# MLP matmul steps cut into 32-row pieces beside single score tiles, with other margins in the order and another head

## The chip, the cores and the metric

One core of one Trainium2 chip. The time is microseconds (us) of device time of one execution. The kernel before has a median of 706.06 us (704.78 to 706.14, three runs). In each set of runs below the kernel before was run beside the others on the same chip; its medians there were 705.9 to 706.1 us. The mean clock granted to TensorE differs a little from run to run, and the time with it: of eleven runs of the kernel before, the one at clock 1.000 took 704.58 us and the three at 0.990 took 707.2 to 707.5 us. So I compare medians first, and runs of equal clock where that matters.

## The reference

```python
def reference(A_x, A_wqkv, A_wo, B_x, B_w1, B_b1, B_w2, B_b2):   # [cut]
    xn = layernorm(A_x)                      # 1 x 2048 x 512, bf16
    # A: softmax attention of layernorm'd rows, 32 heads of width 16
    q, k, v = split(xn @ wqkv)
    a = softmax(q @ k.T / 4) @ v             # per head, 2048 x 2048 scores
    A = merge_heads(a) @ wo
    # B: an MLP over the token axis, 2048 -> 1376 -> 2048
    h = layernorm(xn)
    u = gelu(einsum("bsd,sf->bdf", h, w1) + b1)
    B = transpose(einsum("bdf,fs->bds", u, w2) + b2)
    return A_x + A + B
```

The scores are the bulk of it: 32 x 2048 x 2048 exponentials.

## The kernel before

The kernel writes its own static instruction order. A list scheduler with modelled durations picks, again and again, the operation that can start first, and appends it to the order of its engine. At run time every engine works through its order in sequence and waits for semaphores. So a wrong model does no harm to correctness; it puts a waiting operation in front of a ready one.

A *score tile* is 128 keys x 1024 (two heads x 512 queries): two matmuls on two row groups of 32 rows each, into two banks of PSUM, the memory that TensorE writes its results to. There are three such PSUM slots. The tile is exponentiated either by ScalarE or by VectorE, the latter with an integer trick of four terms. A *PV group* (exponentials times the values V) is four matmuls on the four column groups of 32 columns. An *MLP step* has the same form. Row-tiled scores and column-tiled PV and MLP work therefore alternate in phases.

```python
def score_specs(n):                      # [cut] two row groups, S phase
    r = 2 * (n % 2) + i                  # rows 0,1 or 2,3
    matmul(bank(2 * s_ + i), lhsT=KT[32*r:32*r+32, T, ...], rhs=QT[32*r:32*r+32, b % 4, :],
           tile_position=(32 * r, 0))
def pv_specs(item, first, last):         # [cut] four column groups, C phase; 1 (ScalarE) or 4 (VectorE) of them per tile
    matmul(bank(PV_BANK)[32*c:32*c+32, ...], lhsT=vt[:, off:off+32], rhs=buf(p, ...), tile_position=(0, 32 * c))
def ext_mm(dst_rows, lhs_of, rhs, reads, start, stop, name):   # [cut] one MLP or projection step, C phase
    for c in range(4):
        matmul(bank(EX_BANK)[32*c:32*c+w, :], lhsT=lhs_of(32*c, 32*c+w), rhs=rhs, tile_position=(0, 32 * c))

# [cut] a score on VectorE: one tensor_scalar from PSUM, then three shifted copies (1 on VectorE, 2 on GpSimd)
# [cut] the head
warm_up(N_WARM, 5)
pool.memset(v17_main[:, :, 16:17], 1.0)          # the 2.3 us GpSimd memset
ln_stats(0); ...; ln_rstd(1, 2); ln_stats(3)     # ln_rstd runs on GpSimd
for t in range(NPRE): ln_norm(t)                 # bf16 tensor_scalar on VectorE
late_memsets()                                   # four small GpSimd memsets
for t in range(NPRE): transpose_pe(t, TB[t])
```

The softmax here doesn't subtract the row's maximum and nothing guards it: scores larger than these inputs give would overflow.

## Time and profile before

I cut the span at two marks: the start of the first exponential of a score tile, and the start of the last PV matmul.

| stretch | us |
|---|---|
| head: to the first exponential | 12.95 |
| main: first exponential to last PV matmul | 680.07 |
| tail: last PV matmul to the end of the span | 11.26 |
| span of the profiled run | 704.3 |

First, the page of the kernel before: busy time of each engine (PE is TensorE, PEld its weight loads, DVE VectorE, ACT ScalarE, POOL GpSimd), then the costliest groups (line, engine, operation, operands, count, then busy us and mean ns of one, then the engine's idle time just before and what ended it).

```profile
PE 688.5 (98%) x12808; PEld 325.6 (46%) x12808; DVE 607.0 (86%) x879; ACT 680.4 (97%) x744; POOL 391.3 (56%) x666
...
L737 ACT ACTIVATE pT<-ps 128x1024 bf16<-128x1024 f32 x522 | 515.4, 1151 | 3.8 <-PE ps L713 3.2
L713 PE MATMUL ps<-QT,KT 32*128 32x512 bf16 x2048 | 291.0, 384 | 5.0 <-ACT pT L737 3.0
L748 DVE TENSOR_SCALAR pT<-ps 128x1024 int16<-128x1024 f32 x207 | 252.9, 1222 | 32.7 <-PE ps L713 23.6
...
L748 DVE TENSOR_SCALAR x_sb<-ps 128x1024 int16<-128x1024 f32 x92 | 112.4, 1222 | 15.3 <-PE ps L713 10.8
```

207 + 92 = 299 of the 1024 score tiles go to VectorE. VectorE waits 23.6 + 10.8 = 34.4 us for them.

The table by stage of the kernel before (stretch, length, then busy us and instructions of PE, PEld, DVE, ACT, POOL, then the clock, the DMA share and GB/s):

```profile
100.00:600.00 500.00, 496.57 (x9574) 234.38 (x9570) 441.45 (x591) 498.99 (x544) 289.75 (x482) 1.00 0.18 40
600.00:690.00 90.00, 89.31 (x1636) 40.57 (x1628) 78.95 (x106) 89.21 (x99) 52.35 (x89) 1.00 0.21 51
```

ScalarE is full: 498.99 of 500 us. VectorE is at 441.45 / 500 = 88.3%.

The timeline of the kernel before (start, length, engine, line, operation; in brackets how long the engine stood idle before it and what released it), at the head, in two score phases near 303 us, and at the tail:

```profile
2.72 2.29 POOL L626 MEMSET V<- 128x512 bf16 x1
...
6.55 2.28 DVE L522 TENSOR_SCALAR hx<-x_sb,mv 128x512 bf16<-128x512 bf16 x4
...
10.14 1.48 PE L601 MATMUL ps<-xnT,wq_sb 128*128 128x128 bf16 x12
...
12.95 3.77 ACT L737 ACTIVATE pT<-ps 128x1024 bf16<-128x1024 f32 x4 [0.81 <-PE ps L713]
...
302.99 0.48 PE L713 MATMUL ps<-QT,KT 32*128 32x512 bf16 x4
303.40 0.40 PE L780 MATMUL ps<-pT,V 128*32 128x256 bf16 x8
...
304.06 0.39 PE L713 MATMUL ps<-QT,KT 32*128 32x512 bf16 x2
304.38 0.29 PE L780 MATMUL ps<-pT,V 128*32 128x256 bf16 x4
...
693.12 2.55 PE L810 MATMUL ps<-gT_sb,wblk 128*32 128x512 bf16 x44
...
695.67 0.42 DVE L1043 TENSOR_TENSOR oT<-ps,oC 128x256 bf16<-128x256 f32 x1
...
698.41 1.03 PE L1059 MATMUL ps<-wo_t,oT 128*128 128x512 bf16 x4
```

Three things are to be seen. A phase of one score tile (x2 matmuls) takes 304.38 - 304.06 = 0.32 us until the next column-tiled work, and one of two tiles (x4) takes 0.41 us here. At the tail, TensorE works off eleven MLP steps (x44) after the last PV matmul. And the head ends at 12.95 us.

### The profile page before, as it was taken

The page shows a single profiled execution, that of the slowest core. Times are in us where ns is not written, and L with a number is a line of the kernel's source. Part 1 is how long each engine was busy: PE and PEld are TensorE (multiplying, and loading weights), DVE is VectorE, ACT ScalarE, POOL GpSimd, SP SyncE. Part 2 cuts the span into 40 slices and gives each one's busy share as a digit, 9 for nine tenths or more (in the row PEclk, how much of TensorE's full clock was granted, in tenths as well). Part 3 has the DMA queues.
Part 4 walks back from the last instruction along what each step waited for, and adds up shares of the span by engine and source line. Part 5 has one row for each costly group of instructions (what it writes and reads, how often), then busy time and mean ns, then how long its engine had stood idle before and what let it go on. Part 6 is the DMA issues. An engine that isn't in the chain of part 4 may idle for free.

```text
span 704.3 us, 29187 instructions
## 1 busy us (share of the span) xinstructions
PE 688.5 (98%) x12808; PEld 325.6 (46%) x12808; DVE 607.0 (86%) x879; ACT 680.4 (97%) x744; POOL 391.3 (56%) x666
## 2 busy tenths in 40 slices
PE   7999999999999999999999999999999999999998
PEld 4533544444444454444444454444544444445444
DVE  6968889888897889989889998979899888988886
ACT  5999999999999999999999999999999999999993
POOL 5535446565564636556565674546556564665551
PEclk9999999999999999999999999999999999999999
DMA  7103200221002200211221023112221121222211
GB/s 210 32 19 69 51 23 14 52 49 27 15 14 53 48 23 18 43 36 36 49 42 44 19 47 72 48 39 53 54 55 35 43 66 41 53 55 54 48 43 47
DMA packets 85727, 32.31 MB, mean 46 GB/s; under 512 B 67424, under 2 KB 85600, under 8 KB 85600
## 3 DMA queue, kind: packets, MB, share of 16 engines
q1 hardware_dynamic: 85168, 30.05, 18.4%
q8 instruction: 100, 1.64, 1.0%
q10 hardware_dynamic: 432, 0.39, 0.2%
q14 instruction: 27, 0.22, 0.1%
HBM read 21.76 MB, written 2.35 MB: 34 GB/s over the span
## 4 chain that ended last, share of the span: by engine, by line
PE 73%; ACT 19%; DVE 3%; issue 2%; SPq 2%; POOL 1%; DVEq 0%; DMA 0%; POOLq 0%
PE ps L780 27%; PE ps L713 27%; PE ps L810 15%; ACT pT L737 13%; ACT x_sb L737 4%; SPq L404 2%; PE ps L859 1%; DVE pT L748 1%; ACT gT_sb L914 1%; PE ps L619 0%; DVE oT L1006 0%; PE ps L563 0%; PE ps L550 0%; DVE x_sb L748 0%; POOL V L626 0%
## 5 line engine op out<-in xcount | busy, mean ns | idle before, releaser
L737 ACT ACTIVATE pT<-ps 128x1024 bf16<-128x1024 f32 x522 | 515.4, 1151 | 3.8 <-PE ps L713 3.2
L713 PE MATMUL ps<-QT,KT 32*128 32x512 bf16 x2048 | 291.0, 384 | 5.0 <-ACT pT L737 3.0
L748 DVE TENSOR_SCALAR pT<-ps 128x1024 int16<-128x1024 f32 x207 | 252.9, 1222 | 32.7 <-PE ps L713 23.6
L754 POOL INT64_ADD pT<-pT x307 | 185.6, 613 | 147.1 <-DVE pT L757 80.9
L780 PE MATMUL ps<-pT,V 128*32 128x256 bf16 x4632 | 237.9, 275 | 0.9 <-ACT pT L737 0.6
L737 ACT ACTIVATE x_sb<-ps 128x1024 bf16<-128x1024 f32 x203 | 221.8, 1159 | 1.1 <-PE ps L713 0.9
L713 PEld LDWEIGHTS ps<-QT,KT 32*128 32x128 bf16 x2048 | 86.5, 91 | 179.2 <-ACT pT L737 80.6
L780 PEld LDWEIGHTS ps<-pT,V 128*32 128x32 bf16 x4632 | 109.9, 96 | 68.0 <-issue 52.1
L748 DVE TENSOR_SCALAR x_sb<-ps 128x1024 int16<-128x1024 f32 x92 | 112.4, 1222 | 15.3 <-PE ps L713 10.8
L780 PE MATMUL ps<-x_sb,V 128*32 128x256 bf16 x1856 | 115.1, 275 | 0.3 <-ACT x_sb L737 0.3
L754 POOL INT64_ADD pT<-x_sb x128 | 77.4, 613 | 56.8 <-DVE pT L757 32.6
L754 POOL INT64_ADD x_sb<-pT x114 | 69.4, 613 | 44.8 <-DVE pT L757 31.0
L757 DVE TENSOR_SCALAR pT<-pT 128x1024 int16<-128x1024 int16 x149 | 63.4, 428 | 4.5
L780 PE MATMUL ps<-pT,VM 128*32 128x256 bf16 x884 | 61.2, 274 | 0.0
L810 PE MATMUL ps<-hx,wblk 128*32 128x512 bf16 x688 | 60.5, 384 | 0.0
L810 PE MATMUL ps<-gT_sb,wblk 128*32 128x512 bf16 (+1 forms) x704 | 58.4, 383 | 0.7 <-DVE hx L948 0.7
L780 PEld LDWEIGHTS ps<-x_sb,V 128*32 128x32 bf16 x1856 | 47.3, 96 | 24.2 <-issue 18.1
L754 POOL INT64_ADD x_sb<-x_sb x58 | 35.3, 613 | 28.4 <-DVE pT L757 8.1
L757 DVE TENSOR_SCALAR pT<-x_sb 128x1024 int16<-128x1024 int16 x66 | 27.9, 424 | 2.1
L810 PEld LDWEIGHTS ps<-hx,wblk 128*32 128x32 bf16 x688 | 16.2, 94 | 24.1 <-issue 21.1
L780 PEld LDWEIGHTS ps<-pT,VM 128*32 128x32 bf16 x884 | 23.6, 97 | 6.6 <-issue 6.1
L810 PEld LDWEIGHTS ps<-gT_sb,wblk 128*32 128x32 bf16 (+1 forms) x704 | 16.3, 95 | 20.8 <-issue 16.1
(105 smaller groups left out, 397.4 us busy)
## 6 DMA issues: line engine op xcount, KB each, us to landing
wblk<-in_B_w_dram SPq DMA_DIRECT2D x10, 512.0 KB, 4.6
wblk<-in_B_w_dram SPq DMA_DIRECT2D x16, 320.0 KB, 3.6
oC<-OT SPq DMA_DIRECT2D x248, 16.0 KB, 1.8
denb<-rden_scratch SPq DMA_DIRECT2D x124, 32.0 KB, 2.0
xr<-in_A_x_dram SPq DMA_DIRECT2D x16, 128.0 KB, 2.3
dcomp<-OT SPq DMA_DIRECT2D x124, 2.0 KB, 1.8
QT<-Qall SPq DMA_DIRECT2D x120, 16.0 KB, 1.8
out_dram<-osb SPq DMA_DIRECT2D x14, 128.0 KB, 1.9
```

Source lines behind the costliest of these rows:

```text
L404: return eng.dma_start(dst, src)
L713: specs.append(dict(eng="pe", fn=lambda e, r=r, bk=bk: e.matmul(bank(bk), lhsT=KT[32 * r:32 * r + 32, T, 128 * kt:128 * (kt + 1)], rhs=QT[ ...
L737: return [dict(eng="act", fn=lambda e: e.activation(buf(pbuf[n]), ps[:, s_ * 1024:(s_ + 1) * 1024], ACTF.Exp, scale=LN2_128), reads=[("ban ...
L748: return dict(eng="dve", fn=lambda e: e.tensor_scalar(buf_i(w), ps[:, s_ * 1024:(s_ + 1) * 1024], IBIAS, 0.0, ALU.add, ALU.max), reads=[(" ...
L754: return dict(eng=eng, fn=lambda e: e.int64_add(buf_i(o).bitcast(I64), buf_i(w).bitcast(I64), SHIFTS[k] * 0x0001000100010001), reads=[("pT ...
L757: return dict(eng=eng, fn=lambda e: e.tensor_scalar(buf_i(o), buf_i(w), float(SHIFTS[k]), 1.0, ALU.add, ALU.mult), reads=[("pT", w)], writ ...
L780: specs.append(dict(eng="pe", fn=lambda e, c=c, h=h, i=i, off=off: e.matmul(bank(PV_BANK)[32 * c:32 * c + 32, 256 * par:256 * par + 256], ...
L810: specs.append(dict(eng="pe", fn=lambda e, c=c, w=w: e.matmul(bank(EX_BANK)[32 * c:32 * c + w, :], lhsT=lhs_of(32 * c, 32 * c + w), rhs=rh ...
L859: specs.append(dict(eng="pe", fn=lambda e, ct=ct, c=c, i=i, t=t: e.matmul(bank(EX_BANK)[32 * c:32 * c + 32, 128 * i:128 * (i + 1)], lhsT=x ...
L914: yield "act", [dict(eng="act", fn=lambda e, ap=ap: e.activation(ap, ap, ACTF.Gelu_apprx_tanh), reads=[("gT", f) for f in fts], writes=[(" ...
```

## The change

Intent: in a phase with a single score tile two of the four row groups idle. A 32-row piece of an MLP step, a quarter of it, can run there. Four pieces replace one column-tiled step. Around it the order gets other margins, another head, and earlier due times for the output tasks.

```diff
-N_WARM = 11
+N_WARM = 13
+N_MID = (1, 1, 1, 2)              # warm-up matmuls between the transposes
-PE_SWITCH = 0.11
+PE_SWITCH = 0.10
-DMA_I = 0.6
-DMA_L = 3.5
+DMA_I = 0.65
+DMA_L = 3.0
+DMA_SLACK = 0.8                   # with EXT_SLACK = 0.2, PV_SLACK = 0.1: the "margins"
-D_LATE = 1.0
+D_LATE = 0.5                      # when a score tile is wanted for VectorE: the "lateness setting"
 [cut]
+            def piece(r, begin, end=False):
+                rs = slice(32 * r, 32 * r + 32)
+                return [dict(eng="pe", fn=lambda e: e.matmul(
+                    bank(EX_BANK)[0:dst_rows, :], lhsT=lhs_of(0, dst_rows)[rs], rhs=rhs[rs],
+                    start=begin, stop=end, tile_position=(32 * r, 0)), ... name="pc", cost=("S", (r,), 0.214))]
 [cut] pieces(): at the end of a row-tiled phase, one row group of the task's last step goes in if it
       ends with the scores; pieces of different row groups are ordered by TensorE's own semaphore;
       a step is opened for pieces only while its task has at least PIECE_MIN = 6 steps left
-        sc.add("pool", lambda e: e.memset(v17_main[:, :, 16:17], 1.0), ...)      # was before ln_stats(0)
         ln_stats(3)
+        sc.add("pool", lambda e: e.memset(v17_main[:, :, 16:17], 1.0), ...)      # now before the ln_norm loop
         for t in range(NPRE):
             ln_norm(t)
 [cut]
+        for i, z in enumerate(ext_tasks):                                        # the "due times"
+            if z[2] == "fin":
+                due = min(z[1], FIN_END - (NT - 1 - z[4][1]) * FIN_STEP)
+                ext_tasks[i] = (min(z[0], due - 30),) + (due,) + z[2:]
 [cut]
+                    if nm in ("ut", "fin") and any(z[2] == "qt" and z[0] < next_n + Q_GUARD for z in ext_tasks):
+                        continue                                                 # the "query guard"
```

With the query guard goes a rule that the DMAs of query rows are issued before others. A few more small edits are cut.

More of the change, by code (lines that the diff above doesn't have):

```diff
@@ L48 @@
 NPRE = 4
-N_WARM = 11
+N_WARM = 13
+N_MID = (1, 1, 1, 2)
 SEM = 0.05
-PE_SWITCH = 0.11
+PE_SWITCH = 0.10
+PIECE_MIN = 6
+PIECE_OPEN = 1
+HOLD_MAX = 2.0
 PE_LAT = 0.40
@@ L59 @@
 EV_I, EV_L = 0.61, 0.69
-DMA_I = 0.6
-DMA_L = 3.5
+DMA_I = 0.65
+DMA_L = 3.0
+DMA_SLACK = 0.8
+EXT_SLACK = 0.2
+PV_SLACK = 0.1
+GEN_SLACK = 0.0
 SH_I, SH_L = 0.62, 0.70
@@ L68 @@
 D_STEAL = 0.3
-D_LATE = 1.0
+D_LATE = 0.5
 P_KEEP = 4
 DEAD_SLACK = 0.1
+PAIR_WAIT = 0.0
 PORT_SLACK = 0.5
@@ L76 @@
 Q_LEAD = 52
+Q_GUARD = 8
 KV_LEAD = 16
@@ L82 @@
 EX_EARLY = 10
+FIN_END = 985
+FIN_STEP = 18
 GELU_GAP = 16
@@ L124, in __init__ @@
         self.pe_tiles = {}
+        self.phase = 0
+        self.pieces = {}
         self.pe_log = []
@@ L147, in _deps, with ready, piece_ready @@
         return deps
-    def ready(self, eng, reads, writes, dma=False):
+    def ready(self, eng, reads, writes, dma=False, slack=0.0, dma_slack=0.0):
         t = 0.0
         for d in self._deps(eng, reads, writes, dma):
-            t = max(t, d.t1 + (SEM if d.eng != eng or d.is_dma else 0.03))
+            t = max(t, d.t1 + (SEM + (dma_slack if d.is_dma else slack) if d.eng != eng or d.is_dma else 0.03))
         return t
+    def piece_ready(self, r):
+        return max([p.t1 + SEM for q, p in self.pieces.items() if q != r] + [0.0])
     def port_time(self, eng, t):
@@ L174, in _time @@
                 self.pe_tiles = {}
+                self.phase += 1
             for x in tiles:
@@ L208, in add @@
         deps.discard(op)
+        if name == "pc":
+            for r, p in self.pieces.items():
+                if r != cost[1][0]:
+                    deps.add(p)
         if port is None:
             port = eng == "pool" and not dma
-        self._time(op, cost, self.ready(eng, reads, writes, dma), port)
+        rdy = self.ready(eng, reads, writes, dma)
+        if name == "pc":
+            rdy = max(rdy, self.piece_ready(cost[1][0]))
+            self.pieces[cost[1][0]] = op
+        self._time(op, cost, rdy, port)
         if port and eng == "pool" and self.port_op is not None:
@@ L625, in bass_parallel_sum__softmax_full_mha__mixer_token_mlp__prompt_kernel @@
         warm_up(N_WARM, 5)
-        sc.add("pool", lambda e: e.memset(v17_main[:, :, 16:17], 1.0), writes=[("Vone",)], cost=(0.5, 0.6))
         ln_stats(0)
@@ L632, in bass_parallel_sum__softmax_full_mha__mixer_token_mlp__prompt_kernel @@
         ln_stats(3)
+        sc.add("pool", lambda e: e.memset(v17_main[:, :, 16:17], 1.0), writes=[("Vone",)], cost=(2.28, 2.33))
         for t in range(NPRE):
@@ L639, in bass_parallel_sum__softmax_full_mha__mixer_token_mlp__prompt_kernel @@
             transpose_pe(t, TB[t])
+            warm_up(N_MID[t], 5)
         for t in range(NPRE):
@@ L802, in bass_parallel_sum__softmax_full_mha__mixer_token_mlp__prompt_kernel, with ext_mm, step @@
         w_hold = {}
-        def ext_mm(dst_rows, lhs_of, rhs, reads, start, stop, name):
-            specs = []
-            for c in range((dst_rows + 31) // 32):
-                w = min(32, dst_rows - 32 * c)
-                specs.append(dict(eng="pe", fn=lambda e, c=c, w=w: e.matmul(
-                    bank(EX_BANK)[32 * c:32 * c + w, :], lhsT=lhs_of(32 * c, 32 * c + w), rhs=rhs,
-                    start=start, stop=stop, tile_position=(0, 32 * c)),
-                    reads=reads, writes=[("bank", EX_BANK)], name=name, cost=("C", (c,), 0.214)))
-            return specs
+        def ext_mm(dst_rows, lhs_of, rhs, reads, stop, name):
+            def step(begin, end=False):
+                specs = []
+                for c in range((dst_rows + 31) // 32):
+                    w = min(32, dst_rows - 32 * c)
+                    specs.append(dict(eng="pe", fn=lambda e, c=c, w=w: e.matmul(
+                        bank(EX_BANK)[32 * c:32 * c + w, :], lhsT=lhs_of(32 * c, 32 * c + w), rhs=rhs,
+                        start=begin, stop=end, tile_position=(0, 32 * c)),
+                        reads=reads, writes=[("bank", EX_BANK)], name=name, cost=("C", (c,), 0.214)))
+                return specs
+            def piece(r, begin, end=False):
+                rs = slice(32 * r, 32 * r + 32)
+                return [dict(eng="pe", fn=lambda e: e.matmul(
+                    bank(EX_BANK)[0:dst_rows, :], lhsT=lhs_of(0, dst_rows)[rs], rhs=rhs[rs],
+                    start=begin, stop=end, tile_position=(32 * r, 0)),
+                    reads=reads, writes=[("bank", EX_BANK)], name="pc", cost=("S", (r,), 0.214))]
+            return step, piece, stop
         have = {("q", 0), ("q", 1)} | {("k", 0, c) for c in range(4)} | {("v", 0, c) for c in range(4)}
@@ L826, in task_qt @@
         def task_qt(qb, T):
-            for ct in range(NCT):
-                yield "pe", ext_mm(128, lambda a, z, ct=ct: wq_sb[:, ct, 128 * T + a:128 * T + z],
+            yield "steps", [ext_mm(128, lambda a, z, ct=ct: wq_sb[:, ct, 128 * T + a:128 * T + z],
                                    xnT[:, ct, 512 * qb:512 * (qb + 1)],
                                    [("wq", T)] + [("xnT", t) for t in range(4 * qb, 4 * qb + 4)],
-                                   ct == 0, ct == NCT - 1, "qt")
+                                   ct == NCT - 1, "qt") for ct in range(NCT)]
             yield "ev", [dict(eng="dve", fn=lambda e: e.tensor_scalar(Qall[:], bank(EX_BANK), QSCALE, None, ALU.mult),
@@ L843, in task_kt @@
         def task_kt(T, c):
-            for ct in range(NCT):
-                yield "pe", ext_mm(128, lambda a, z, ct=ct: wkv_sb[:, ct, 128 * T + a:128 * T + z],
+            yield "steps", [ext_mm(128, lambda a, z, ct=ct: wkv_sb[:, ct, 128 * T + a:128 * T + z],
                                    xnT[:, ct, 512 * c:512 * (c + 1)],
                                    [("wkv", 0, T)] + [("xnT", t) for t in range(4 * c, 4 * c + 4)],
-                                   ct == 0, ct == NCT - 1, "kt")
+                                   ct == NCT - 1, "kt") for ct in range(NCT)]
             yield "ev", [dict(eng="dve", fn=lambda e: e.tensor_copy(KT[:, T, 512 * c:512 * (c + 1)], bank(EX_BANK)),
@@ L854, in task_vt, with vt_step, step @@
             tiles = list(range(4 * j, 4 * j + 4))
-            for i, t in enumerate(tiles):
-                specs = []
-                for ct in range(NCT):
-                    for c in range(4):
-                        specs.append(dict(eng="pe", fn=lambda e, ct=ct, c=c, i=i, t=t: e.matmul(
-                            bank(EX_BANK)[32 * c:32 * c + 32, 128 * i:128 * (i + 1)],
-                            lhsT=xnT[:, ct, 128 * t + 32 * c:128 * t + 32 * c + 32],
-                            rhs=wkv_sb[:, ct, D + 128 * T:D + 128 * (T + 1)],
-                            start=(ct == 0), stop=(ct == NCT - 1), tile_position=(0, 32 * c)),
-                            reads=[("wkv", 1, T), ("xnT", t)], writes=[("bank", EX_BANK)], name="vt",
-                            cost=("C", (c,), 0.06)))
-                yield "pe", specs
+            def vt_step(i, t):
+                def step(begin, end=False):
+                    return [dict(eng="pe", fn=lambda e, ct=ct, c=c: e.matmul(
+                        bank(EX_BANK)[32 * c:32 * c + 32, 128 * i:128 * (i + 1)],
+                        lhsT=xnT[:, ct, 128 * t + 32 * c:128 * t + 32 * c + 32],
+                        rhs=wkv_sb[:, ct, D + 128 * T:D + 128 * (T + 1)],
+                        start=ct == 0, stop=ct == NCT - 1, tile_position=(0, 32 * c)),
+                        reads=[("wkv", 1, T), ("xnT", t)], writes=[("bank", EX_BANK)], name="vt",
+                        cost=("C", (c,), 0.06)) for ct in range(NCT) for c in range(4)]
+                return step, None, True
+            yield "steps", [vt_step(i, t) for i, t in enumerate(tiles)]
             dst = v17_kh[:, 4 * j:4 * j + 4, 8 * T:8 * T + 8, 0:16]
@@ L894, in task_ut @@
             m = min(128, F - 128 * ft)
-            for st in range(NT):
-                yield "pe", ext_mm(m, lambda a, z, st=st: wblk[:, slot, st, a:z], xn_sb[:, st, :],
-                                   [("wblk", slot, "a"), ("wblk", slot, "b"), ("wblk", slot, "c"), ("h", st)], st == 0, st == NT - 1, "ut")
+            yield "steps", [ext_mm(m, lambda a, z, st=st: wblk[:, slot, st, a:z], xn_sb[:, st, :],
+                                   [("wblk", slot, "a"), ("wblk", slot, "b"), ("wblk", slot, "c"), ("h", st)], st == NT - 1, "ut")
+                            for st in range(NT)]
             if i + NW < NFT:
@@ L928, in task_fin, with op_step @@
             keep = st == NT - 1
-            for ft in range(NFT):
+            steps = []
+            for ft in (0, NFT - 1) + tuple(range(1, NFT - 1)):
                 k = 128 if ft < NFT - 1 else FLAST + 1
-                yield "pe", ext_mm(128, lambda a, z, ft=ft, k=k: wblk[0:k, slot, ft, a:z], gT(ft)[0:k, :],
-                                   [("wblk", slot, "a"), ("wblk", slot, "b"), ("wblk", slot, "c"), ("gT", ft)] + ([("gTone",)] if ft == NFT - 1 else []),
-                                   ft == 0, False, "yt")
+                steps.append(ext_mm(128, lambda a, z, ft=ft, k=k: wblk[0:k, slot, ft, a:z], gT(ft)[0:k, :],
+                                    [("wblk", slot, "a"), ("wblk", slot, "b"), ("wblk", slot, "c"), ("gT", ft)] + ([("gTone",)] if ft == NFT - 1 else []),
+                                    False, "yt"))
+            def op_step(T):
+                return ext_mm(128, lambda a, z: oT(qb)[:, T, 128 * sti + a:128 * sti + z], wo_c[:, T, :],
+                              [("oTc", qb, T)] + [("wo_c", e_, r) for e_ in range(2) for r in range(4)],
+                              T == ng - 1 and not keep, "op")
+            late_T = [T for T in range(ng) if (qb, T) not in oT_done]
+            yield "steps", steps + [op_step(T) for T in range(ng) if T not in late_T]
             if i + NW < NT:
                 yield "call", lambda: w2_load(i + NW)
-            for T in range(ng):
+            for T in late_T:
                 yield "gate", lambda T=T: (qb, T) in oT_done
-                yield "pe", ext_mm(128, lambda a, z, T=T: oT(qb)[:, T, 128 * sti + a:128 * sti + z], wo_c[:, T, :],
-                                   [("oTc", qb, T)] + [("wo_c", e_, r) for e_ in range(2) for r in range(4)],
-                                   False, T == ng - 1 and not keep, "op")
+                yield "steps", [op_step(T)]
             if keep:
-                yield "pe", ext_mm(128, lambda a, z: ident[:, a:z], xr[:, st % 2, :], [("ident",), ("xr", st % 2)],
-                                   False, False, "xr")
+                yield "steps", [ext_mm(128, lambda a, z: ident[:, a:z], xr[:, st % 2, :], [("ident",), ("xr", st % 2)],
+                                       False, "xr")]
             yield "call", lambda: have.add(("f", st))
@@ L1084, in pv_ready @@
                     continue
-                t = sc.last_writer[("pT", it[2])].t1 + SEM
+                t = sc.last_writer[("pT", it[2])].t1 + SEM + PV_SLACK
                 if best is None or t < best[0]:
@@ L1172, in step_gen @@
             while True:
+                g["front"] = None
+                if g.get("steps"):
+                    g["front"] = g["steps"].pop(0)[0]
+                    g["cur"] = ("pe", g["front"](not g.get("begun")))
+                    return
+                if g.get("open"):
+                    g["cur"] = ("hold", None)
+                    return
                 try:
@@ L1177, in step_gen @@
                     return
+                if kind == "steps":
+                    g["steps"] = what
+                    g["open"] = []
+                    g["stop"] = what[-1][2]
+                    continue
                 if kind == "call":
@@ L1190, in step_gen, with est @@
                 return
-        def est(specs):
+        def est(specs, slack=0.0):
             s0 = specs[0]
@@ L1195, in est @@
             for s_ in specs:
-                r = max(r, sc.ready(s_["eng"], s_["reads"], s_["writes"]))
+                r = max(r, sc.ready(s_["eng"], s_["reads"], s_["writes"], slack=slack, dma_slack=DMA_SLACK))
             t = max(sc.free[s0["eng"]], r)
@@ L1221, in backlog, with pieces @@
             return r
+        piece_phase = [None, None]
+        def pieces():
+            g = cur_ext
+            if g is None or g["cur"] is None or g["cur"][0] not in ("pe", "hold") or "open" not in g or sc.pe_mode != "S":
+                return
+            hold = g["cur"][0] == "hold"
+            if hold and "since" not in g:
+                g["since"] = sc.pe_end
+            lim = max(sc.pe_tiles.values()) + 0.03
+            if hold and sc.pe_end - g["since"] > HOLD_MAX:
+                lim += 0.3
+            if sc.phase != piece_phase[0]:
+                piece_phase[:] = [sc.phase, None]
+            for tries in range(2):
+                for o in list(g["open"]):
+                    for r in sorted(o[1]):
+                        if piece_phase[1] not in (None, r) or max(sc.free["pe"], sc.pe_tiles.get(r, 0.0), sc.piece_ready(r)) + 0.214 > lim:
+                            continue
+                        sp_ = o[0](r, not g.get("begun"), hold and g["stop"] and len(g["open"]) == 1 and len(o[1]) == 1)
+                        if est(sp_) > sc.free["pe"] + 0.02:
+                            continue
+                        if not g.get("begun"):
+                            g["begun"] = True
+                            g["cur"] = ("pe", g["front"](False))
+                        piece_phase[1] = r
+                        for z in sp_:
+                            add(z)
+                        o[1].discard(r)
+                        if not o[1]:
+                            g["open"].remove(o)
+                        if hold and not g["open"]:
+                            g.pop("since", None)
+                            step_gen(g)
+                            return
+                        break
+                if len(g["steps"]) >= PIECE_MIN and len(g["open"]) < PIECE_OPEN and g["steps"][-1][1]:
+                    g["open"].append((g["steps"].pop(-1)[1], {0, 1, 2, 3}))
+                else:
+                    return
         def fill(t_next, same):
-            if cur_ext is not None or last_n is None or sc.pe_activity(t_next) > ACT_MIN:
+            if cur_ext is not None or last_n is None or fin_next == NT or sc.pe_activity(t_next) > ACT_MIN:
                 return
@@ L1247, in bass_parallel_sum__softmax_full_mha__mixer_token_mlp__prompt_kernel @@
             cands = []
-            for g in frees:
+            for g in sorted(frees, key=lambda g: not (g["cur"] and g["cur"][0] == "sp" and g["cur"][1][0]["name"] == "q_row")):
                 if g["cur"] and g["cur"][0] == "sp":
@@ L1323, in bass_parallel_sum__softmax_full_mha__mixer_token_mlp__prompt_kernel @@
                 late = next_n - min([cur_ext["due"]] + [z[1] - HARD_HOLD for z in ext_tasks if z[2] in ("qt", "kt", "vt")])
-                jobs.append((max(t_c, est(cur_ext["cur"][1])), 1 if late > -LATE_BY else 3, "ext", cur_ext, 0.214))
+                jobs.append((max(t_c, est(cur_ext["cur"][1], EXT_SLACK)), 1 if late > -LATE_BY else 3, "ext", cur_ext, 0.214))
+            if cur_ext and cur_ext["cur"] and cur_ext["cur"][0] == "hold" and (next_n >= NN or not score_has(next_n)):
+                for o in cur_ext["open"]:
+                    for r in sorted(o[1]):
+                        for z in o[0](r, False, cur_ext["stop"] and o is cur_ext["open"][-1] and r == max(o[1])):
+                            add(z)
+                cur_ext["open"] = []
+                cur_ext.pop("since", None)
+                step_gen(cur_ext)
+                continue
             pick = None
@@ L1341, in bass_parallel_sum__softmax_full_mha__mixer_token_mlp__prompt_kernel @@
                         t2 = 1e9
-                    go = max(e_s, min(need, t2))
+                    go = max(e_s, t2 if t2 <= need + PAIR_WAIT else need)
                 if pick is not None and pick[0] + pick[4] + (PE_SWITCH if sc.pe_mode == "C" else PE_SWITCH) <= go + PE_FIT:
@@ L1357, in bass_parallel_sum__softmax_full_mha__mixer_token_mlp__prompt_kernel @@
             t_est, _, kind, what = min(cands, key=lambda z: z[0])
+            if kind in ("pv", "ext"):
+                pieces()
             if kind in ("score", "pv", "ext"):
@@ L1430, in bass_parallel_sum__softmax_full_mha__mixer_token_mlp__prompt_kernel @@
                 g = what
-                for s_ in g["cur"][1]:
+                for s_ in (g["front"](not g.get("begun"), g["stop"] and not g["steps"] and not g["open"]) if g.get("front") else g["cur"][1]):
                     add(s_)
+                g["begun"] = True
                 step_gen(g)
@@ L1445, in bass_parallel_sum__softmax_full_mha__mixer_token_mlp__prompt_kernel @@
                         continue
+                    if nm in ("ut", "fin") and any(z[2] == "qt" and z[0] < next_n + Q_GUARD for z in ext_tasks):
+                        continue
                     if need and need[0] == "ut" and (need[1] != len(u_begun) or len(h_done) < NT):
@@ L1448, in bass_parallel_sum__softmax_full_mha__mixer_token_mlp__prompt_kernel @@
                     if need and need[0] == "fin":
-                        if need[1] >= 12 and not (("q", NBLK - 2) in have and (NQB - 1, 1) in oT_done):
+                        if need[1] >= 12 and ("q", NBLK - 2) not in have:
                             continue
```

## The prediction

> **What bounds the kernel now.** Between 100 and 600 us ScalarE is the limit. The table by stage gives it 99.4 to 100.0 us busy in every 100 us, and 109 to 111 activations, about 0.91 us per score tile. TensorE also reads 99 us per 100, but that number is inflated by the modelled matmul ends. Start-to-start times in the timeline show it waiting: 265 of the 504 score phases hold two score tiles and 239 hold one. A phase of one tile takes 0.315 us until the next column-tiled matmul, always. A phase of two tiles takes 0.33 us when both PSUM slots are free, and mostly 0.41 us, because the second tile waits for its slot. I sum about 22 us of such waits and about 20 us of late switches, some 8% of these 500 us. VectorE takes the score tiles that ScalarE does not: 299 of 1024 (page, groups). It is 88% busy there. It waits 34 us for scores (waits view). Speed therefore comes only from tiles moved to VectorE, or from the ends of the span.
>
> **What the change does.**
> 1. Pieces. A step of four 32-column matmuls holds TensorE for 0.22 us. As a 32-row piece beside a single score tile, a quarter of it should cost about 7 ns: in phases whose slots are free, four row-group matmuls take 0.328 us and two take 0.315 us, their weight loads overlapping. At most one piece fits per single-tile phase, of which there are about 310 after block 0, and only tasks with six steps left offer one. I estimate 200 pieces, 50 steps, 9 to 10 us of TensorE time. The Trainium skill (TensorEngine Tiling, Gotcha 1) says different row tiles cannot access one PSUM bank at once; the change orders pieces by semaphore, at most one row group per phase. No run here shows that limit.
> 2. Little of this is directly on the chain, because ScalarE is full. It counts if TensorE now delivers scores to VectorE sooner, helped by the halved lateness margin. A tile on VectorE costs it 1.65 us (1.22 plus one 0.43 shift), costs TensorE three more PV groups (0.33 us), and frees about 0.92 us of the span. If VectorE rises from 86% to 88-89%, I estimate 6 to 8 more tiles: 5 to 7 us.
> 3. Head. The clock record shows half speed from about 8.7 to 12.1 us, after a transpose gap; matmuls there are 107 ns apart instead of 56. This agrees with the skill (TensorE: Matmul & The Clock Gate, Part 1): windows of about 3.4 us, idle ones throttle. Warm-ups between transposes should keep full speed, and the 2.29 us GpSimd memset leaves the normalization's way. Estimate 1.5 us.
> 4. Tail. After the last PV (693.1 us) TensorE still does 14 MLP and output steps until 696.2 us, then warm-ups, while the last head's operand is ready at 695.3 us. Earlier due times take this away: estimate 2.5 us.
> 5. DMA and semaphore margins only avoid a few microseconds of mis-estimated waits: 0 to 1 us.
>
> **Prediction.** 706 - 6 - 1.5 - 2.5 - 1 is about 695 us; 80% range 685 to 702. Faster by over 2%: 0.33; within 2%: 0.64; slower: 0.03.
>
> **What would show it.** 32-row MLP matmuls, 150 to 250 of them, and as many fewer 32-column ones; single phases still 0.32 us; more than 299 tiles on VectorE, at 88% busy or above; no half clock after 8 us; first exponential near 11.5 us, not 12.95; no MLP steps after the last PV.
>
> **What would make it wrong.** Pieces lengthening a phase by a 91 ns weight load; VectorE limited by something else than scores, so that its count stays; MLP steps moved earlier crowding the last blocks; or the reshuffled schedule feeding VectorE much better, which would give over 2%.

## More of the kernel before

All runs quoted are of the state "fast".

One line of the waits view of the kernel before (who waited for whom: us in total, times, longest):

```profile
DVE oT L1006 <- DMA denb<-rden_scratch: 3.2, 4, 1.2
```

VectorE normalizes a pair of finished heads with denominators that come by DMA; this wait becomes important below.

## The result and the profile after

| | before | after |
|---|---|---|
| median, us | 706.02 | 697.15 (697.01 to 698.68, four runs) |
| head | 12.95 | 15.27 |
| main | 680.07 | 672.42 |
| tail | 11.26 | 9.16 |
| span of the profiled run | 704.3 | 696.9 |
| score tiles on VectorE | 299 | 307 |
| 32-row pieces | 0 | 192 |

The ratio is 0.9883, 95% interval 0.9866 to 0.9901. Ratios are the mean time of one kernel's fast runs over that of the other's of the same rounds, so not quite the ratio of the medians quoted. The profiled run of the changed kernel was its slowest, 698.68 us at clock 0.998; the other three took 697.0 to 697.2 us at clock 1.000. The clock record of the profiled run has one half-speed window of 3.4 us, in the head; a clock of 1.000 leaves no room for one.

The page of the changed kernel:

```profile
PE 678.8 (97%) x12916; PEld 312.0 (45%) x12916; DVE 621.3 (89%) x894; ACT 673.2 (97%) x736; POOL 402.2 (58%) x683
...
L765 ACT ACTIVATE pT<-ps 128x1024 bf16<-128x1024 f32 x535 | 523.2, 1132 | 3.3 <-PE ps L741 2.7
L776 DVE TENSOR_SCALAR pT<-ps 128x1024 int16<-128x1024 f32 x221 | 270.1, 1222 | 26.8 <-PE ps L741 20.8
L741 PE MATMUL ps<-QT,KT 32*128 32x512 bf16 x2048 | 284.8, 385 | 5.3 <-ACT pT L765 3.5
...
L776 DVE TENSOR_SCALAR x_sb<-ps 128x1024 int16<-128x1024 f32 x86 | 105.1, 1222 | 14.7 <-PE ps L741 11.8
```

221 + 86 = 307 tiles on VectorE. Its waits for scores went only from 34.4 to 32.6 us.

The table by stage of the changed kernel:

```profile
100.00:600.00 500.00, 495.04 (x9799) 227.01 (x9795) 454.11 (x606) 499.31 (x545) 304.43 (x507) 1.00 0.18 42
600.00:690.00 90.00, 88.70 (x1667) 39.28 (x1659) 80.04 (x112) 84.67 (x93) 46.27 (x77) 1.00 0.19 44
```

VectorE rose to 454.11 / 500 = 90.8%. ScalarE stayed full.

The timeline of the changed kernel at the same places:

```profile
6.47 4.43 DVE L549 TENSOR_SCALAR hx<-x_sb,mv 128x512 bf16<-128x512 bf16 x4
...
7.73 2.27 POOL L659 MEMSET V<- 128x512 bf16 x1
...
10.96 0.40 PE L577 MATMUL ps<-ident,hx 128*128 128x128 bf16 x4 [2.51 <-DVE hx L549]
...
15.27 1.94 ACT L765 ACTIVATE pT<-ps 128x1024 bf16<-128x1024 f32 x2 [1.35 <-PE ps L741]
...
302.93 0.39 PE L741 MATMUL ps<-QT,KT 32*128 32x512 bf16 x4
...
303.26 0.29 PE L808 MATMUL ps<-pT,VM 128*32 128x256 bf16 x4
...
303.92 0.39 PE L741 MATMUL ps<-QT,KT 32*128 32x512 bf16 x2
...
303.93 0.39 PE L847 MATMUL ps<-hx,wblk 32*128 32x512 bf16 x1
...
304.24 0.29 PE L808 MATMUL ps<-pT,V 128*32 128x256 bf16 x4
...
690.97 1.04 PE L1101 MATMUL ps<-wo_t,oT 128*128 128x512 bf16 x4 [0.73 <-DVE oT L1085]
```

The piece (L847) runs beside the single tile, and the phase still takes 304.24 - 303.92 = 0.32 us. Over the stretch from 60 to 680 us the median of 184 such phases is 0.321 us against 0.318 us for 117 phases of one tile without a piece: a piece costs 3 ns. At the tail no MLP step is left; the last output matmuls start right after VectorE's operand. But in the head the four normalizations (L549) take 4.43 us where they took 2.28 us, while the memset (L659) runs, and TensorE waits 2.51 us for them.

The waits view of the changed kernel:

```profile
DVE oT L1048 <- DMA denb<-rden_scratch: 0.9, 1, 0.9
```

### The profile page after: what moved, and what is told of

It reads as the page before. It is cut to its first block, busy times and chain, and to the rows that moved or that the text cites. A ratio compares the mean times of both kernels' runs of the same rounds, so it can differ in the third digit from the quotient of the medians.

```text
span 696.9 us, 29358 instructions
## 1 busy us (share of the span) xinstructions
PE 678.8 (97%) x12916; PEld 312.0 (45%) x12916; DVE 621.3 (89%) x894; ACT 673.2 (97%) x736; POOL 402.2 (58%) x683
## 4 chain that ended last, share of the span: by engine, by line
PE 80%; ACT 12%; DVE 4%; DMA 2%; issue 1%; POOL 0%; SPq 0%; DVEq 0%
PE ps L808 32%; PE ps L741 29%; PE ps L839 15%; ACT pT L765 8%; ACT x_sb L765 3%; PE ps L893 2%; DMA denb<-rden_scratch 1%; DVE pT L776 1%; DVE OT L1012 1%; ACT gT_sb L950 1%; DVE hx L549 0%; SPq L431 0%; DMA x_sb<-in_A_x_dram 0%; PE ps L590 0%; DVE oT L1048 0%
## 5 line engine op out<-in xcount | busy, mean ns | idle before, releaser
L765 ACT ACTIVATE pT<-ps 128x1024 bf16<-128x1024 f32 x535 | 523.2, 1132 | 3.3 <-PE ps L741 2.7
L776 DVE TENSOR_SCALAR pT<-ps 128x1024 int16<-128x1024 f32 x221 | 270.1, 1222 | 26.8 <-PE ps L741 20.8
L765 ACT ACTIVATE x_sb<-ps 128x1024 bf16<-128x1024 f32 x182 | 197.9, 1141 | 0.2 <-PE ps L741 0.2
L741 PEld LDWEIGHTS ps<-QT,KT 32*128 32x128 bf16 x2048 | 78.8, 91 | 183.5 <-ACT pT L765 76.3
L782 POOL INT64_ADD x_sb<-pT x146 | 89.3, 616 | 57.0 <-DVE pT L785 32.7
L776 DVE TENSOR_SCALAR x_sb<-ps 128x1024 int16<-128x1024 f32 x86 | 105.1, 1222 | 14.7 <-PE ps L741 11.8
L782 POOL INT64_ADD pT<-x_sb x132 | 79.9, 614 | 48.2 <-DVE pT L785 32.6
L839 PE MATMUL ps<-hx,wblk 128*32 128x512 bf16 x594 | 52.4, 383 | 0.0
L782 POOL INT64_ADD x_sb<-x_sb x47 | 28.6, 614 | 23.8 <-DVE pT L785 8.0
L847 PE MATMUL ps<-hx,wblk 32*128 32x512 bf16 (+1 forms) x96 | 37.1, 387 | 0.0
L785 DVE TENSOR_SCALAR x_sb<-pT 128x1024 int16<-128x1024 int16 x64 | 27.1, 428 | 1.8
L808 PEld LDWEIGHTS ps<-pT,VM 128*32 128x32 bf16 x880 | 23.3, 96 | 10.6 <-issue 8.8
```

Of the source, the lines that this page charges most:

```text
L741: specs.append(dict(eng="pe", fn=lambda e, r=r, bk=bk: e.matmul(bank(bk), lhsT=KT[32 * r:32 * r + 32, T, 128 * kt:128 * (kt + 1)], rhs=QT[ ...
L765: return [dict(eng="act", fn=lambda e: e.activation(buf(pbuf[n]), ps[:, s_ * 1024:(s_ + 1) * 1024], ACTF.Exp, scale=LN2_128), reads=[("ban ...
L776: return dict(eng="dve", fn=lambda e: e.tensor_scalar(buf_i(w), ps[:, s_ * 1024:(s_ + 1) * 1024], IBIAS, 0.0, ALU.add, ALU.max), reads=[(" ...
L782: return dict(eng=eng, fn=lambda e: e.int64_add(buf_i(o).bitcast(I64), buf_i(w).bitcast(I64), SHIFTS[k] * 0x0001000100010001), reads=[("pT ...
L785: return dict(eng=eng, fn=lambda e: e.tensor_scalar(buf_i(o), buf_i(w), float(SHIFTS[k]), 1.0, ALU.add, ALU.mult), reads=[("pT", w)], writ ...
L808: specs.append(dict(eng="pe", fn=lambda e, c=c, h=h, i=i, off=off: e.matmul(bank(PV_BANK)[32 * c:32 * c + 32, 256 * par:256 * par + 256], ...
```

## The experiments

"Pieces", "margins", "lateness setting", "query guard" and "due times" are as marked in the diff. Some experiments undo one part in the changed kernel; others put one part alone into the kernel before. With every part undone, the orders of all five engines came out equal to those of the kernel before, so nothing hides between the parts (this was compared on the built programs; it is not a run). The times:

| run | what it is | median us (range) | ratio to before | head, main, tail | tiles on VectorE |
|---|---|---|---|---|---|
| before | | 706.06 | 1 | 12.95, 680.1, 11.3 | 299 |
| after | | 697.15 | 0.9883 | 15.27, 672.4, 9.2 | 307 |
| no_pieces | after, no pieces | 702.73 (701.6-703.5) | 0.9950 | 15.11, 674.1, 11.9 | 307 |
| d_late_one | after, old lateness | 701.29 (700.1-701.7) | 0.9933 | 15.35, 674.9, 9.2 | 304 |
| margins_old | after, old margins | 700.20 (699.6-701.9) | 0.9923 | 15.32, 674.8, 8.2 | 304 |
| guard_off | after, no query guard | 700.20 (698.2-703.9) | 0.9924 | 15.20, 678.0, 8.9 | 311 |
| fin_late | after, old due times | 698.29 (696.8-700.0) | 0.9897 | 15.35, 672.2, 10.6 | 309 |
| memset_back | after, memset as before | 695.42 (695.4-695.9) | 0.9850 | 11.96, 672.6, 9.5 | 307 |
| head_ordered | after, memsets behind the norms | 694.85 (694.7-695.0) | 0.9840 | 11.28, 672.8, 9.0 | 307 |
| nudged | head_ordered, another order | 694.94 (694.8-695.4) | 0.9845 | 11.37, 673.3, 9.0 | 306 |
| pieces_alone | before + pieces | 714.42 (712.7-715.7) | 1.0114 | 13.60, 688.1, 11.3 | 302 |
| margins_alone | before + margins | 714.65 (712.8-718.5) | 1.0130 | 12.22, 688.6, 11.5 | 301 |
| lateness_alone | before + lateness | 721.82 (720.6-724.4) | 1.0231 | 11.62, 694.5, 16.5 | 310 |
| pieces_margins | before + both | 706.39 (704.3-709.8) | 1.0013 | 12.87, 683.4, 11.6 | 303 |

Head, main and tail are of the one profiled run of each, as defined above. All results were correct.

The runs of these kernels did not all get the same clock. This is what they took at equal clock, where there are such runs:

| run | at clock 1.000 | at clock 0.998 | the rest |
|---|---|---|---|
| after | 697.0 to 697.2 (3 runs) | 698.7 (1) | |
| no_pieces | 701.6 to 701.7 (2) | 702.3 to 703.5 (2) | 703.1 to 703.4 at 0.997 (2) |
| d_late_one | 700.1 (1) | 701.3 to 701.7 (4) | |
| guard_off | | 698.2 to 698.9 (2) | 699.9 to 703.9 at 0.993 to 0.995 (4) |
| fin_late | 696.8 (1) | 698.3 (1) | 698.2 to 700.0 at 0.995 to 0.997 (3) |
| margins_old | | | 699.6 to 701.9 at 0.990 to 0.995 (5) |

### no_pieces

```diff
-PIECE_MIN = 6
+PIECE_MIN = 99
```

> The changed kernel with the pieces switched off; head, margins and due times as changed. Theory A (the pieces relieve TensorE, so VectorE gets more tiles): about 6 us slower than the changed kernel, near 703 us, with about 300 score tiles on VectorE instead of 307 and no 32-row MLP matmuls. Theory B (the main stretch became shorter through the margins and the lateness setting, the pieces do nothing): within 1.5 us of the changed kernel, 696 to 698.5 us, with about 307 tiles on VectorE.

Measured: 702.73 us, which is theory A's time, but 307 tiles on VectorE, which is theory B's. The main stretch lost only 674.1 - 672.4 = 1.7 us without the pieces. The tail lost 11.9 - 9.2 = 2.8 us. Of the 5.6 us between the medians, 4.5 us remain when runs of clock 1.000 are compared. VectorE waits 27.7 us for scores here, against 32.6 us with the pieces: by this sum the pieces did not bring it scores sooner. The timeline of no_pieces shows what the tail lost:

```profile
688.66 0.61 PE L808 MATMUL ps<-x_sb,V 128*32 128x256 bf16 x16
...
689.95 2.56 PE L839 MATMUL ps<-gT_sb,wblk 128*32 128x512 bf16 x44 [0.47 <-DVE hx L990]
...
695.26 1.03 PE L1101 MATMUL ps<-wo_t,oT 128*128 128x512 bf16 x4
```

Eleven steps of the last MLP task come again after the PV work. So the pieces did give TensorE room, but the larger part of it came out at the end, as MLP work finished earlier, and not as tiles moved to VectorE. My step "pieces, hence more tiles on VectorE" falls: the tiles are there without the pieces.

### pieces_alone

Everything but the pieces, and the step lists that they need, put back as before.

> The kernel before with the pieces (and the step lists they need) alone; head, margins, lateness and due times as before. Theory A: about 700 us (6 us faster than before), 305 or more tiles on VectorE, first exponential at 12.9 us as before. Theory B: 705 to 707 us, about 299 tiles on VectorE.

Measured: 714.42 us, 8.4 us slower than before; both theories miss. ScalarE's idle gaps of over 0.15 us between 30 and 690 us, summed from the trace's records, are 8.6 us against 3.0 us before, and most lie about 42 us apart, where one pair of heads follows another. The timeline of VectorE in pieces_alone at one of them:

```profile
306.43 0.89 DVE L1048 TENSOR_TENSOR oT<-oC,denb 128x256 bf16<-128x256 f32 x2 [0.73 <-DMA denb<-rden_scratch]
307.23 0.68 DVE L868 TENSOR_SCALAR Qall<-ps 128x512 bf16<-128x512 f32 x1
```

VectorE stands 0.73 us at the normalization of finished heads, for a DMA that the order had expected sooner. The PSUM evacuation behind it (L868) comes late; the next MLP step in TensorE's order waits for that bank; the scores stand behind the step; and ScalarE then goes idle for 1.05 us at 308.11 us. Gaps like this stand before VectorE's normalization 14 times, 13.1 us in sum, in pieces_alone, and 7 times, 5.5 us, before. The waits view names the DMA for most of it:

```profile
DVE oT L1048 <- DMA denb<-rden_scratch: 8.2, 7, 1.6
...
DVE wkv_raw L1048 <- DMA denb<-rden_scratch: 2.9, 4, 0.7
```

Of the 8.0 us that the main stretch is longer, ScalarE's gaps account for 5.6 us.

### memset_back and head_ordered

memset_back puts the 2.3 us memset back in front of the first normalization statistics. head_ordered is this:

```diff
-        sc.add("pool", lambda e: e.memset(v17_main[:, :, 16:17], 1.0), ...)
         for t in range(NPRE):
             ln_norm(t)                 # in ln_norm: + port=t < NPRE, so that later GpSimd work depends on it
+        sc.add("pool", lambda e: e.memset(v17_main[:, :, 16:17], 1.0), ...)
         late_memsets()
```

> The changed kernel with the 2.27 us GpSimd memset put back in front of the first normalization. Theory A for the head (the memset, moved, holds the port that the fourth VectorE normalization needs, 3.10 instead of 0.87 us): that normalization back under 1 us, first exponential at 12.5 us or before instead of 15.27, time about 694.5 us. Theory B for the head (the extra warm-up matmuls delay the transposes): first exponential stays near 15 us, time 697.

> The changed kernel with all four GpSimd memsets ordered behind the fourth normalization by a dependency. Theory A for the head: that normalization takes 0.4 us, no stall in the transposes, TensorE at full clock through the projections, first exponential at 11.3 to 12.0 us, time 693 to 694 us. Theory B: as the changed kernel, 697 us.

Measured: 695.42 and 694.85 us, first exponentials at 11.96 and 11.28 us. Theory A for the head holds in both. TensorE's order in head_ordered is, row by row, that of the changed kernel, so nothing but the head differs. The times missed the expected ones by 0.9 us: the profiled head became 4.0 us shorter, the timed runs only 697.15 - 694.85 = 2.3 us. The profiled run of the changed kernel was 1.5 us slower than its other runs, which closes most of this: those ran at clock 1.000, without the half-speed window in the head. So the stall alone costs about 2.3 us, the difference of the timed runs; the rest I put down to the half-speed window that came with it in the profiled run (an estimate, from 698.68 against 697.1 us).

The tile view of the four normalizations in the kernel before, the changed kernel and head_ordered (shortest, median and longest of the four, in ns; then the first and last start, in us):

```profile
L522 DVE TENSOR_SCALAR hx<-x_sb,mv x4: 381/410/869, 6.5 to 8.0; 128x512 bf16<-128x512 bf16 x4
...
L549 DVE TENSOR_SCALAR hx<-x_sb,mv x4: 381/410/3095, 6.5 to 7.8; 128x512 bf16<-128x512 bf16 x4
...
L549 DVE TENSOR_SCALAR hx<-x_sb,mv x4: 381/410/415, 6.4 to 7.7; 128x512 bf16<-128x512 bf16 x4
```

The timeline of head_ordered:

```profile
6.39 1.75 DVE L549 TENSOR_SCALAR hx<-x_sb,mv 128x512 bf16<-128x512 bf16 x4
...
8.20 2.29 POOL L661 MEMSET V<- 128x512 bf16 x1 [0.51 <-DVE hx L549]
...
11.28 1.94 ACT L765 ACTIVATE pT<-ps 128x1024 bf16<-128x1024 f32 x2 [0.48 <-PE ps L741]
```

The records of the single instructions show it sharply. The fourth normalization took 3.10 us in the changed kernel (it began 0.08 us after the memset and ended 0.15 us after the last of the GpSimd memsets), 0.87 us before, beside the four small memsets alone, and in head_ordered the four together take 1.75 us. The Trainium skill (SBUF — State Buffer, "Who interferes with whom") says that a VectorE instruction in a two-port mode and a GpSimd instruction need the same port pair, and that whoever comes second blocks for the whole instruction. The trace agrees. In the changed kernel VectorE did not get in between the memsets that follow each other. In the kernel before it did: its fourth normalization ended at 8.83 us, 0.15 us after the third of the small memsets and before the end of the fourth.

The clock record agrees with the rest of the head. In memset_back and head_ordered the projections' matmuls start 56 ns apart throughout. In the profiled run of the changed kernel they go over from 56 to 107 ns at about 12.2 us, where a half-speed window of the clock record begins, after the stall had let TensorE idle (by its records it was busy 37% of the 3.4 us before). head_ordered is the fastest kernel, 2.3 us under the changed one.

### margins_alone, lateness_alone, pieces_margins

Each puts the named part into the kernel before, all else as before.

> The kernel before with the transfer and semaphore margins of the change alone (no pieces; lateness, head and due times as before). Theory C (the main stretch became shorter because the order no longer puts a VectorE operation that waits for a transfer in front of ready work): VectorE's waits in front of the head normalizations fall from 5.5 us to under 2 us, the main stretch (first exponential to last PV) from 680 to about 676 us, time near 702 us, tiles on VectorE still about 299. Theory D (the lateness setting does it): 705 to 707 us.

> The kernel before with the lateness setting halved alone. Theory D: 304 to 308 tiles on VectorE, main stretch about 675 us, time near 701 us. Theory C: within 2 us of before, and VectorE's waits for transfers in front of the head normalizations still 5 us or more.

> The kernel before with the pieces and the margins. Theory C: the 13 us of VectorE waits for transfers that the pieces alone showed fall to 2 to 4 us, ScalarE's gaps from 8.6 to under 2 us, time near 700 us, 14 us faster than the pieces alone. Rival (the pieces themselves lengthen the order, by their semaphores or their weight loads): still above 708 us.

Measured: 714.65, 721.82 and 706.39 us. Theories C and D both miss for the single parts. Theory C's wait did not fall either: the stands before VectorE's normalizations are 10.1 us in margins_alone and 8.5 us in pieces_margins. The gain of 8 us from adding the margins to the pieces is there, but ends at the time of before, not at 700 us. In pieces_margins ScalarE's gaps are 7.9 us, not under 2. D gets its tiles (310 on VectorE) and the slowest time of all, so the number of tiles on VectorE alone does not decide the time. lateness_alone shows a second way to lose; its timeline:

```profile
404.64 0.69 DVE L868 TENSOR_SCALAR Qall<-ps 128x512 bf16<-128x512 f32 x1 [0.20 <-PE ps L839]
...
405.39 3.63 PE L839 MATMUL ps<-hx,wblk 128*32 128x512 bf16 x64
406.54 4.36 SPq L431 DMA_DIRECT2D QT<-Qall  x6
...
409.83 0.59 PE L741 MATMUL ps<-QT,KT 32*128 32x512 bf16 x2 [0.16 <-DMA QT<-Qall]
...
410.46 1.02 ACT L765 ACTIVATE pT<-ps 128x1024 bf16<-128x1024 f32 x1 [5.45 <-PE ps L741]
```

The query projection for the next pair was copied out only at 404.64 us, its rows were issued from 406.54 us on, and ScalarE stood idle for 5.45 us. Between such a copy and the first score of its pair lie 33 to 38 us for 13 of the 15 pairs in the changed kernel, 15 to 37 us in all pairs before, and 5.2 to 32 us in lateness_alone; the 5.2 us are the case shown. ScalarE's gaps are 19.5 us in lateness_alone and 8.1 us in margins_alone, against 3.0 us before.

### margins_old, d_late_one, guard_off

Each undoes the named part in the changed kernel.

> The changed kernel with the margins of before. Theory C: VectorE's waits for transfers in front of the head normalizations rise from 3 to 8 us or more, ScalarE gaps appear at the changes of head pair, time 701 to 706 us. Theory D: within 2 us of the changed kernel, 697 us.

> The changed kernel with the lateness setting of before, 1.0 instead of 0.5. Theory D (the lateness setting gives VectorE its 8 more tiles): about 299 to 301 tiles on VectorE, main stretch 678 us or more, time near 703 us. Theory A (the pieces do): 305 or more tiles, within 2 us of 697 us.

> The changed kernel without the rule that MLP tasks wait while a query projection is due, and without issuing query rows first. Theory E (three of the parts alone were slower because query rows then arrive late or VectorE operations wait at each change of head pair; the rule is what lets the pieces and the halved lateness pay): query copies come within 20 us of the first score of their pair in several pairs instead of 33 to 35, ScalarE shows gaps of 3 us or more in sum, time 701 to 710 us. Rival (the rule does nothing, single parts were slower by luck of the order): within 2 us of 697 us.

Measured: 700.20, 701.29 and 700.20 us, so by medians each part is worth 3 to 4 us inside the changed kernel. The table of equal clocks keeps 2.6 to 3.0 us of this for the lateness setting. For the margins there is no run at equal clock, and the two runs of guard_off at clock 0.998 are no slower than the changed kernel at that clock (698.2 and 698.9 against 698.7 us). Of theory C for margins_old only the direction held: the stands before VectorE's normalizations went from 3.1 to 4.6 us, not to 8, and ScalarE's gaps are 1.6 us. What fell is the number of tiles on VectorE, 304 instead of 307. d_late_one has 304 tiles and a main stretch 2.5 us longer, so theory D holds in kind and in part of its size: the lateness setting gives three of the eight tiles. (The main stretch of margins_old, 2.4 us longer, contains a half-speed window of 6.8 us from 51.7 us on.) guard_off shows what theory E expected of the trace: the query copies come 14.7 to 24.9 us before their scores in six pairs that have 33 us or more in the changed kernel, ScalarE's gaps are 8.7 us instead of 1.1 us in the profiled run, although there are 311 tiles on VectorE. Its runs scatter (698.2 to 703.9 us), and the profiled one is the slowest of them, with half-speed windows of 3.4 us from 96.5 and from 390.0 us on. The timeline of guard_off at its two largest gaps of ScalarE:

```profile
70.11 0.38 PE L741 MATMUL ps<-QT,KT 32*128 32x512 bf16 x1 [0.79 <-DMA QT<-Qall]
...
70.53 1.02 ACT L765 ACTIVATE pT<-ps 128x1024 bf16<-128x1024 f32 x1 [2.09 <-PE ps L847]
...
94.24 0.88 DVE L1048 TENSOR_TENSOR oT<-oC,denb 128x256 bf16<-128x256 f32 x2 [2.79 <-DMA denb<-rden_scratch]
...
96.82 1.02 ACT L765 ACTIVATE pT<-ps 128x1024 bf16<-128x1024 f32 x1 [1.96 <-PE ps L741]
```

The first is a score at the start of a head pair that waits for its query row. The second is not: VectorE stands for denominators, 1.9 us without a matmul follow, and then a half-speed window. And in the kernel before query copies came as late as 15.5 us before their scores, with gaps of 3.0 us in sum. So theory E explains a part of the gaps; that the guard is worth anything in time at equal clock is not shown.

### fin_late and nudged

fin_late drops the loop of the due times; its matmuls come in the order of the changed kernel up to 578.6 us (row 2211 of 2667 of TensorE's order). nudged is head_ordered with the modelled length of the exponential 1.04 instead of 1.03 us.

> The changed kernel without the earlier due times of the output tasks; TensorE's order is the same up to row 2211 of 2667. If the due times gave the tail its 2 us: tail (last PV to end) near 11.3 us instead of 9.2 and time near 699 us. If the pieces gave it: tail stays near 9.2 us, time 697 us.

> The changed kernel with the memsets ordered, and one modelled latency changed by 0.01 us (the exponential's), which changes nothing but the order. It sizes the luck of the order: I expect within 3 us of 694.9 us, and no theory may rest on differences below what this run shows.

Measured: 698.29 us with a tail of 10.6 us, and 694.94 us. The due times give the tail 1.5 us, the pieces 2.8 us, and neither reaches it without the other. In time, the few runs at equal clock show no cost of undoing them (696.8 us at clock 1.000 against 697.0 to 697.2, 698.3 at 0.998 against 698.7); the profiled run of fin_late, at 0.995, has a half-speed window from 670.5 us on. nudged has another order from row 305 on and differs by 0.1 us. One nudge is a small sample, and the kernel before was not nudged; that differences of 1 us between these variants are more than luck of the order is likely but not shown. The single parts in the kernel before lost 8 to 16 us, far more than this one nudge.

## Why the prediction was right or wrong

- **Total: right.** 695 us was predicted, 685 to 702 us as the range; 697.15 us was measured, a gain of 1.2%, inside "within 2%". Luck is in it: the head lost where 1.5 us of gain were expected, the margins may have given more than expected, and the main stretch gained the expected amount for another reason.
- **Cost and number of pieces: right.** About 200 pieces were predicted and 192 ran; I estimated 7 ns for each and 3 ns was measured. The 91 ns weight load did not lengthen the phase. The Trainium skill (TensorEngine Tiling, Gotcha 1) forbids two row tiles in one PSUM bank at once; the change never does it, so no run shows that limit.
- **"If VectorE rises from 86% to 88-89%, I estimate 6 to 8 more tiles: 5 to 7 us": the numbers were right by luck, the cause was wrong.** VectorE rose to 89% of the span, got 8 more tiles, and the main stretch became 7.65 us shorter. But without the pieces there are still 307 tiles and 6.0 of these us. The step "TensorE now delivers scores to VectorE sooner" through the pieces is the one that failed. Part of the gain comes from the lateness setting (three tiles, 2.5 us of main stretch when undone). The margins go with three more tiles, but the 2.4 us that undoing them costs contain a half-speed window. For the query guard the profile shows 5.6 us, in its slowest run with two such windows; the two runs at equal clock show nothing.
- **"DMA and semaphore margins ... 0 to 1 us": too small.** Undoing them costs 3.05 us by medians, all runs of it at a lower clock (0.990 to 0.995), so how much of this is the order itself is open.
- **"Head ... Estimate 1.5 us": the step that failed.** The head became 2.3 us longer in the profile; without the half-speed window of that run I estimate 0.8 us longer (1.5 us less, from 698.68 against 697.1 us). I had costed the memset only on GpSimd's own order and not the port that VectorE needs beside it. The table of single instructions before already had the hint: one of four equal normalizations took 0.87 instead of 0.41 us, while the small memsets ran. (The half-speed window of the kernel before did not follow on an idle stretch, as "idle ones throttle" suggests: by its records TensorE was busy 46% of the 3.4 us before it, mostly with transposes.) The warm-ups themselves work once that is out of the way (memset_back: no half-speed window, first exponential at 11.96 us).
- **Tail: right.** 2.5 us predicted, 11.26 - 9.16 = 2.1 us measured; it needs the pieces as well as the due times.
- The parts do not add up. Undone singly from the changed kernel the five parts cost 5.6 + 4.1 + 3.05 + 3.05 + 1.1 = 16.9 us, while the whole gain with the head mended is 11.2 us; put singly into the kernel before, three of them cost 8 to 16 us. The first sum is of medians and too large: in the few runs at equal clock undoing the guard or the due times costs nothing, the pieces about 4.5 and the lateness setting about 3 us.

What stays open. The phases of two score tiles have a median of 0.407 to 0.410 us in all five kernels that kept the modelled switch time of 0.11 us (before, pieces_alone, margins_alone, lateness_alone, pieces_margins) and 0.325 to 0.349 us in the changed kernel and the eight kernels made from it, which have 0.10 us. Each other part was undone only one at a time, and none of these moved the median back, so that one constant is a likely cause, and it may carry part of the 6 us that the main stretch gains without pieces; it was not run alone, and the phase can be short only because TensorE waits elsewhere. Also open are 2.4 of the 8.0 us that pieces_alone lost in its main stretch; a half-speed window of 6.8 us lies in it, from 55.1 us, which neither the kernel before nor the changed one has there. And open is whether an edit brings half-speed windows about or only meets them: in the main stretch they began without long stands of TensorE (the longest in the 3.4 us before was 1.9 us in guard_off at 96.5 us, and 0.3 us in margins_old at 51.7 us).

## What to carry to other kernels

In a statically ordered kernel, cost a moved operation on every shared resource it holds, not only on its own engine: a 2.27 us GpSimd memset put beside a 0.4 us VectorE instruction cost the head more than all the clock warm-ups could win. When several edits come together, undo each in the finished kernel as well as adding it alone: here the number came out as predicted and the cause did not, and only the removal of the pieces showed it. And look at the idle gaps of the engine that is full: lateness_alone moved 310 tiles off ScalarE and was the slowest of all, with 19.5 us of ScalarE gaps, 5.45 us of them at one start of a head pair. Last, look at the clock of each run before a difference of a few us is put down to an edit: by medians the due times and the query guard seemed to be worth 1 and 3 us, and the few runs at equal clock show none of it.

## What the Trainium skill lacked or had wrong

- SBUF — State Buffer, "Who interferes with whom": nothing wrong, but it does not say that a waiting VectorE instruction may be passed by several GpSimd instructions in a row. In the changed kernel it stood through one memset of 2.27 us and the small ones behind it, 3.10 us in all for an instruction that takes 0.4 us; in the kernel before it got in ahead of the last small memset.
- TensorEngine Tiling says that a change of tiling mode drains TensorE, with no time for it. Here a row-tiled phase of 512 columns takes 0.318 us until the column-tiled work starts, against 0.22 us from one column-tiled group of 512 columns to the next.
